# An RWKV-7 and GELU-MLP kernel: the two MLP products in other tile shapes of TensorE

## The chip, the core and the metric

The kernel runs on one core of one Trainium2 chip. The metric is the device time in microseconds of one execution on that core. TensorE does the matrix products into PSUM; VectorE (DVE), ScalarE (ACT) and GpSimd (POOL) do elementwise work; SyncE (SP) issues the DMAs.

## The reference

A recurrence over 768 steps for 4 x 8 heads of 40 channels, then an MLP on the 3072 tokens. All is fp32.

```python
for t in range(S):                       # S = 768; state is (B, H, D, D), D = 40
    y[:, :, t] = einsum('bhd,bhde->bhe', r[t], state)
    Sa = einsum('bhde,bhe->bhd', state, a[t])
    state = state * w[t] - Sa (outer) b[t] + v[t] (outer) k[t]
x = y as (3072 tokens, 320)              # B*S, H*D
h = x @ w_in                             # (3072, 2048)
g = h * (1 / (1 + exp(-1.702 * h)))
out = g @ w_out                          # (3072, 320)
```

## The kernel before

The sequence is cut into 12 chunks of 64 steps. A chunk has two units, each with two batches (p = 0, 1), so there are 24 units. For each unit the attention part forms decays, score products and a triangular solve by six doubling levels (`level`, tiles `ps_level`, `W`, `E`), then the output and the next state. Each level is a product of TensorE, an eviction by ScalarE or VectorE, and the next level waits for it. The unit's output goes through DRAM and comes back as `xT`, the transposed tokens for the MLP: 256 tokens of a chunk, 128 in each half.

The MLP of chunk c (`mlp`, L834) has these steps:

- `up(q, m, k)`: the 2048 hidden channels are 16 blocks of 128; q (four) and m (two) name a pair of blocks, r = 0, 1 one of the pair, and k one of five pieces of 64 of the 320 input channels. `w_in_sb` holds block r of a pair in row half r, and both row halves of `xT` hold the same 64 input channels of all 256 tokens. A task computes both blocks of its pair for one k; each block's 128 columns of weights are cut into two of 64, so that a task is four products of 64 rows by 64 columns with 256 moving columns. Block r has its own PSUM bank. There are 40 tasks a chunk.
- `gelu(q)`: one ScalarE activation of 128x1024 from PSUM into `g`.
- `down(p)`: for p = 0 and then p = 1, eight tasks `part(m)` sum over the 2048 hidden channels. The contraction of 128 rows is cut into two row halves, which go to the two banks of a PSUM pair; the 128 tokens are cut into two column halves. At the end a copy takes the first bank into `ob`, and a VectorE add brings in the second (L871, L873); then `store` issues two DMAs on SP.

In every product of the kernel the array stands as four 64x64 tiles, addressed in the order of `QUARTERS` (L243). A product in fp32 is two pairs of LDWEIGHTS and MATMUL instructions, so a task of four products with its loads has 16 instructions. All matmuls are issued by the helper `mm` (L270, L271 in the profile).

The program's order is written out by a planner (`Plan`, L59). A task has a rank, the engines that can run it and their costs in ns; `order` plays the five engines forward in time and takes for each free engine the ready task of lowest rank. Attention tasks have ranks below those of the MLP (10000 and more), so MLP tasks fill the time in which no attention task is ready. The planner also plays TensorE's instruction fetch in blocks of 256 (`fetched`, `ahead`): if the next task would run too far ahead of the fetch, it prefers a ready task with fewer instructions for its time. `paced` spreads the MLP tasks of a chunk over the time until the next chunk's. PSUM is handed out as four pairs of banks; `pair=(...)` names what holds a pair, and the last reader frees it. The number of buffers of each tile stands in one table (`g=4`, `ob=1`, `xT=3`).

Of the kernel before, what the change touches and what calls it, by code (L numbers as in the profile page):

```python
# [49 lines left out]

class Task:
    def __init__(self, rank, engines, fn, pair, most, size):
        self.instr, self.sbuf = engines.pop("instr", 0), engines.pop("sbuf", False)
        self.rank, self.fn, self.pair, self.most, self.size = rank, fn, pair, most, size
        self.engines = engines
        self.after, self.then, self.release = set(), [], 0.0


class Plan:  # L59
# [5 lines left out]
    BLOCK, FETCH, BESIDE, AHEAD = 256, 3550.0, 0.4, 300.0  # L65
    DELAY = {"PE": 300.0, "DVE": 60.0, "ACT": 60.0, "POOL": 150.0, "SP": 800.0}

    LATENCY, RATE, SPREAD = 1200.0, 400.0, 1.3

    def __init__(self, slots, pairs):  # L70
        self.slots, self.pairs = slots, pairs
# [25 lines left out]
    def order(self):  # L97
# [10 lines left out]
        able, now, wire, out, many = [], 0.0, 0.0, [], set()  # L108
# [8 lines left out]
                return clear > len({o.pair[0] for o in able if o.most is not None and o.pair not in held and not any(k[0] == o.pair[0] for k in many)})  # L117
            return clear > 0 and sum(k[0] == t.pair[0] for k in many) < t.most

        issued, begun, shared = 0, 0.0, 0.0  # L120

        def fetch(at):
            took = self.FETCH
# [9 lines left out]
        def fetched(t, start):  # L133

            at, left, ns, block = start, t.instr, t.engines["PE"] / t.instr, begun
            room = self.BLOCK - issued % self.BLOCK
            while left >= room:
                at += room * ns
                left -= room
                at = block = max(at, block + fetch(block))  # L140
                room = self.BLOCK
            return at + left * ns, block
# [5 lines left out]
        while coming or able:  # L148
            while coming and coming[0][0] <= now:
                able.append(self.tasks[heapq.heappop(coming)[1]])  # L150
            able.sort(key=lambda t: (t.rank, t.n))
            took = None
            for e in free:
                if free[e] <= now:
                    took = next((t for t in able if e in t.engines and fits(t) and unread(t, e) <= now), None)
                    if took and e == "PE" and ahead(took) > self.AHEAD:

                        took = next((t for t in able if e in t.engines and fits(t) and ahead(t) < min(self.AHEAD, ahead(took))), took)
                    if took:
                        break  # L160
            if not took:
                later = [x for x in (*free.values(), *pairs, *(unread(t, e) for t in able for e in t.engines)) if now < x < float("inf")]
                now = min(later + ([coming[0][0]] if coming else []))
                continue
            t = took
            able.remove(t)
            t.engine = e
            end = now + t.engines[e]
            if e == "PE":
                end, begun = fetched(t, now)  # L170
                issued += t.instr
            if e == "POOL" or e == "DVE" and t.sbuf:

                shared = max(now, shared) + t.engines[e]
                end = max(end, shared)
            free[e] = end
            if e == "SP":
                wire = max(wire, end + self.LATENCY)
                running.append((wire, wire + self.SPREAD * t.size / self.RATE))
                end = wire = running[-1][1]  # L180
            if t.pair is not None:
                if e != "PE":
                    last.setdefault(t.pair, {})[e] = end
                if t.pair not in held:
                    held[t.pair] = next(i for i, p in enumerate(pairs) if p <= now)
                    pairs[held[t.pair]] = float("inf")
                    if t.most is not None:
                        many.add(t.pair)
                t.bank = held[t.pair]
                users[t.pair] -= 1  # L190
                if not users[t.pair]:
                    many.discard(t.pair)
                    pairs[t.bank] = end + self.DELAY[e]
            for o in t.then:
                o.ready = max(o.ready, end + (0.0 if o.engines.keys() == {e} else self.DELAY[e]))
                o.left -= 1
                if not o.left:
                    heapq.heappush(coming, (max(o.ready, o.release), o.n))
            t.start = now
            out.append(t)  # L200
# [24 lines left out]
def rwkv7_gelu_quick(ctx: ExitStack, tc: tile.TileContext, time_d, v_d, w_d, wc_d, ak_d, b_d, rv_d, w_in, w_out, out):  # L225
    nc = tc.nc
    H, D, S = 8, 40, out.shape[0] // 4
    DM = H * D
# [3 lines left out]
    PIECE = w_in.shape[2]  # L232
    NF = w_in.shape[0] * PIECE // DM
    NM = NF // 2
    NK = DM // 64
    NQ = NM // 2
# [4 lines left out]
    HALF = [slice(0, 64), slice(64, 128)]  # L241
    BITS = (0, 1)
    QUARTERS = [(0, 0), (1, 1), (0, 1), (1, 0)]  # L243
# [5 lines left out]
    banks = ctx.enter_context(tc.tile_pool(name="banks", bufs=1, space=bass.MemoryType.PSUM))  # L249

    plan = Plan(dict(logw=3, wc=3, G=1, wch=3, wz=2, time=2, ak=2, b=2, rv=2, FT=3, GT=1, kh=2, bh=2, bz=2,
                     A=1, Av=1, RV=2, W=2, W0=2, W1=2, E=2, E0=2, E1=2, edge=1, zraw=2, zT=1, saT=1, M=2, y=1, x=1, xT=3, g=4, ob=1), 4)
    tiles, psums, drams = {}, {}, {}

    def single(name, shape):
# [9 lines left out]
    def psum(t, name):  # L265
        if t.pair not in psums:
            psums[t.pair] = banks.tile([128, 2, 512], FP32, tag=f"pair{t.bank}", name=name)
        return psums[t.pair]

    def mm(o, lhsT, rhs, start):  # L270
        nc.tensor.matmul(o, lhsT, rhs, start=start, stop=True, skip_group_check=True)  # L271
# [5 lines left out]
    def pe(*sets):  # L277

        return {"PE": sum(n * 2 * max(58.0, cols / 1.2 + 3) for n, cols in sets), "instr": sum(16 * n for n, _ in sets)}

    def dve(n):
        return {"DVE": 170.0 + 1.03 * n}
# [4 lines left out]
    def any2(n):  # L287
        return {**act(n), **dve(n)}

    def copy(e):  # L290
        return nc.scalar.copy if e == "ACT" else nc.vector.tensor_copy
# [22 lines left out]
    for p in HALF:  # L314
        q = slice(p.start, p.start + MID)
# [518 lines left out]
    def mlp(c):  # L834
        R = 10000 + 100 * c

        def up(q, m, k):
            def go(t):
                ph, x = psum(t, "ps_up"), xT_of(c)[:, :, k]
                for r, h in QUARTERS:  # L840
                    mm(ph[HALF[h], r, m * 256:(m + 1) * 256], w_in_sb[HALF[r], 2 * q + m, k, h * 64:(h + 1) * 64], x[HALF[r]],
                       m == 0 and k == 0)
            plan.add(R + q, pe((1, 256)), go, reads=[("xs", (c, p)) for p in BITS] + [("weight", q)],
                     uses=[("xT", c)], room=[("g", c * NQ + q)], pair=("up", c * NQ + q), most=1)

        def gelu(q):
            plan.add(-45, act(1024), lambda t: nc.scalar.activation(  # L847
                g_of(c * NQ + q).rearrange("p m r n -> p r m n"), psum(t, "").rearrange("p r (m n) -> p r m n", m=2),
                ACT.Gelu_apprx_sigmoid), writes=[("g", c * NQ + q)], pair=("up", c * NQ + q))

        def down(p):
            serial = 2 * c + p

            def part(m):
                def go(t):
                    po, g = psum(t, "ps_down"), g_of(c * NQ + m // 2)[:, m % 2]
                    for f in (2 * m, 2 * m + 1):
                        for r, b in QUARTERS:
                            o = p * 128 + b * 64
                            mm(po[HALF[b], r, :DM], g[HALF[r], f % 2, o:o + 64], w_out_sb[HALF[r], f * DM:(f + 1) * DM], f == 0)  # L860
                parts = range(2 * m * DM // PIECE, (2 * (m + 1) * DM - 1) // PIECE + 1)
                plan.add(R + 10 * (p + 1) + m, pe((2, 320)), go, reads=[("g", c * NQ + m // 2)] + [("weight", NQ + n) for n in parts],
                         pair=("down", serial), most=1)
            for m in range(NM):
                part(m)

            def store(t):
                for b in BITS:
                    o = (2 * p + b) * S + c * C
                    nc.sync.dma_start(out[o:o + C, :], ob_of(serial)[HALF[b]])  # L870
            plan.add(-45, any2(320), lambda t: copy(t.engine)(ob_of(serial), psum(t, "")[:, 0, :DM]),  # L871
                     writes=[("ob", serial)], pair=("down", serial))
            plan.add(-45, dve(320), lambda t: nc.vector.tensor_add(ob_of(serial), ob_of(serial), psum(t, "")[:, 1, :DM]),  # L873
                     reads=[("ob", serial)], writes=[("out", serial)], pair=("down", serial))
            plan.add(-100, {"SP": 700.0}, store, reads=[("ob", serial), ("out", serial)], size=128 * DM * 4)

        for q in range(NQ):
            for m in BITS:
                for k in range(NK):
                    up(q, m, k)  # L880
            gelu(q)
        for p in BITS:
            down(p)

    for i in range(3):
        load_w(i)
# [105 lines left out]
```

## Time and profile before

| what | value |
|---|---|
| two timed executions | 815.56 and 823.68 us, median 819.62 us |
| span of the profiled execution, first to last instruction | 816.7 us |
| its own time beside the span | not given apart; the span lies between the two timed executions |
| TensorE matmul busy, weight load busy | 749.6 us, 636.1 us, 24192 instructions each |
| VectorE, ScalarE, GpSimd busy | 477.7, 352.3, 153.3 us |
| granted TensorE clock, mean | 0.994 |
| up: matmul records, busy, mean of one | 3840, 274.5 us, 378 ns |
| down: matmul records, busy, mean of one | 3072, 243.8 us, 431 ns |
| instruction fetch (queue 8) | 190 packets, 3.11 MB |

In the profile PE is matmul and PEld is weight load. Matmuls are pipelined: a record's length holds the way through the array, and records of neighbouring matmuls lie over each other, so busy time is more than streaming time. The distance between the starts of successive matmuls on the same tile shows how long one occupies it. "issue" as the end of a wait means that the engine waited for nothing that the profile shows.

### The profile page before, as it was taken

The numbers are of one execution on the slowest core, as the hardware profiler recorded it, in microseconds if no ns is written. First come the engines' busy times: TensorE is split into PE (matmuls) and PEld (weight loads), VectorE is DVE, ScalarE is ACT, GpSimd is POOL, SyncE is SP. The second block draws the span as 40 slices with busy tenths as digits, with TensorE's granted clock in tenths as the row PEclk, the third lists the DMA queues.
The fourth block names the chain that finished last, engine by engine and source line by source line (L and its number), as shares of the span: only waits on it lengthen the run. The fifth ranks groups of instructions, "written<-read, shape, count | busy, mean of one in ns | idle before, by whom it ended". The sixth has DMA issues, their size and how long they took to land.

```text
span 816.7 us, 51357 instructions
## 1 busy us (share of the span) xinstructions
PE 749.6 (92%) x24192; PEld 636.1 (78%) x24192; DVE 477.7 (58%) x764; ACT 352.3 (43%) x603; POOL 153.3 (19%) x209
## 2 busy tenths in 40 slices
PE   4567887999999999999999989999999999999997
PEld 3556766787798888788888888887787887899785
DVE  7489778755755755756755654745556545455200
ACT  4376874444344253245254344355346345243210
POOL 4024052012202302302302302302103213200000
PEclk9899999999999999999999999999999999999999
DMA  9834452223403502412412512412403213110200
GB/s 348 329 110 146 136 194 72 70 69 89 134 17 91 152 20 86 133 45 82 138 45 68 152 44 74 141 46 72 142 15 98 71 50 92 40 33 4 60 10 18
DMA packets 32731, 76.31 MB, mean 93 GB/s; under 512 B 5096, under 2 KB 14312, under 8 KB 31496
## 3 DMA queue, kind: packets, MB, share of 16 engines
q1 hardware_dynamic: 32520, 73.03, 28.7%
q8 instruction: 190, 3.11, 1.6%
q14 instruction: 21, 0.17, 0.1%
HBM read 65.14 MB, written 7.86 MB: 89 GB/s over the span
## 4 chain that ended last, share of the span: by engine, by line
PE 79%; ACT 7%; DVE 6%; issue 4%; DMA 3%; SPq 1%; POOL 0%; ACTq 0%; DVEq 0%; POOLq 0%
PE ps_down L271 24%; PE ps_up L271 22%; PE ps_level L271 17%; PE ps_y L271 4%; PE ps_N L271 2%; ACT W L726 2%; PE ps_saT L271 1%; PE ps_Av L271 1%; PE ps_M L271 1%; PE ps_NT L271 1%; PE ps_A L271 1%; PE ps_RV L271 1%; PE ps_rz L271 1%; ACT L847 1%; PE ps_zT L271 1%
## 5 line engine op out<-in xcount | busy, mean ns | idle before, releaser
L271 PE MATMUL ps_up<-xT,w_sb 64*64 64x256 f32 x3840 | 274.5, 378 | 7.6 <-issue 4.5
L271 PE MATMUL ps_down<-w_sb,g 64*64 64x320 f32 x3072 | 243.8, 431 | 2.9 <-DVE w_sb L406 1.6
L726 ACT COPY W<-ps_level 128x672 f32<-128x672 f32 (+1 forms) x164 | 102.4, 626 | 184.2 <-PE ps_level L271 176.7
L271 PEld LDWEIGHTS ps_up<-xT,w_sb 64*64 64x64 f32 x3840 | 159.9, 134 | 27.3 <-issue 7.2
L271 PEld LDWEIGHTS ps_level<-W,E 64*64 64x64 f32 x5888 | 153.0, 134 | 27.9 <-issue 4.5
L271 PEld LDWEIGHTS ps_down<-w_sb,g 64*64 64x64 f32 x3072 | 130.9, 133 | 43.8 <-DVE w_sb L406 2.0
L271 PE MATMUL ps_level<-W,E 64*64 64x64 f32 (+2 forms) x5888 | 152.2, 230 | 7.8 <-issue 2.5
L721 DVE TENSOR_TENSOR E<-twice,ps_level 128x512 f32<-128x512 f32 x120 | 81.8, 686 | 87.8 <-ACT W L726 75.6
L538 POOL TENSOR_TENSOR kh<-time,G 128x320 f32<-128x320 f32 x23 | 20.8, 906 | 414.5 <-issue 289.3
L271 PE MATMUL ps_level<-W 64*64 64x64 f32 (+2 forms) x2560 | 69.4, 239 | 22.1 <-issue 10.3
L271 PEld LDWEIGHTS ps_level<-W 64*64 64x64 f32 x2560 | 66.2, 138 | 29.5 <-issue 15.0
L847 ACT ACTIVATE g<-ps_up 128x1024 f32<-128x1024 f32 x48 | 49.2, 1026 | 42.6 <-PE ps_up L271 42.2
L812 POOL TENSOR_TENSOR x<-y,FT 128x128 f32<-128x128 f32 x88 | 56.1, 667 | 0.7 <-DVE y L802 0.4
L705 DVE TENSOR_TENSOR W<-edge,ps_level 128x672 f32<-128x672 f32 x40 | 33.9, 850 | 12.2 <-PE ps_level L271 11.1
L530 POOL TENSOR_TENSOR ak<-ak,FT 128x512 f32<-128x512 f32 x20 | 27.9, 1394 | 64.1 <-DMA ak<-in_ak 55.8
L873 DVE TENSOR_TENSOR ob<-ob,ps_down 128x320 f32<-128x320 f32 x24 | 11.6, 482 | 48.0 <-ACT ob L871 45.7
L271 PE MATMUL ps_y<-RV,kh 64*64 64x104 f32 x768 | 37.1, 251 | 1.3 <-issue 1.3
L271 PE MATMUL ps_y<-M,bh 64*64 64x104 f32 x768 | 37.5, 250 | 0.5 <-issue 0.4
L726 DVE COPY W<-ps_level 128x672 f32<-128x672 f32 (+1 forms) x36 | 26.4, 733 | 14.2 <-PE ps_level L271 14.1
L271 PEld LDWEIGHTS ps_y<-RV,kh 64*64 64x64 f32 x768 | 29.0, 133 | 4.6 <-issue 2.9
L767 DVE TENSOR_TENSOR M<-ps_M,upper 128x512 f32<-128x512 f32 x24 | 16.6, 690 | 26.5 <-PE ps_M L271 26.4
L716 DVE TENSOR_TENSOR E<-twice,ps_level 128x256 f32<-128x256 f32 x40 | 16.8, 420 | 26.1 <-ACT W L726 16.9
(114 smaller groups left out, 986.0 us busy)
## 6 DMA issues: line engine op xcount, KB each, us to landing
time<-in_time SPq DMA_DIRECT2D x24, 480.0 KB
xT<-x_dram SPq DMA_DIRECT2D x48, 160.0 KB
ak<-in_ak SPq DMA_DIRECT2D x44, 160.0 KB
rv<-in_rv SPq DMA_DIRECT2D x44, 160.0 KB
wc<-in_wc SPq DMA_DIRECT2D x24, 264.0 KB
extra<-in_w_out SPq DMA_DIRECT2D x4, 1280.0 KB
logw<-in_w SPq DMA_DIRECT2D x24, 160.0 KB
RV<-in_v SPq DMA_DIRECT2D x24, 160.0 KB
```

The source lines that it names most:

```text
L271: nc.tensor.matmul(o, lhsT, rhs, start=start, stop=True, skip_group_check=True)
L530: plan.add(R, {"DVE": 690.0, "POOL": 1270.0, "sbuf": True}, lambda t: of(t.engine).tensor_mul(ahT(), ahT(), FT_of(i)), reads=T("ak", "FT") ...
L538: plan.add(R + 4, {"POOL": 870.0, "DVE": 490.0, "sbuf": True}, lambda t, n=n, dst=dst: of(t.engine).tensor_mul(dst(i)[:, :, :D], by_head(t ...
L705: plan.add(key, dve(672), lambda t: nc.vector.tensor_sub(W_of(s + 2)[:, :, b], edge[:, :, b], item(t)[:, :, :, :168]), reads=T("edge"), wr ...
L716: plan.add(key, dve(256), lambda t: nc.vector.tensor_tensor(E_of(es + 2)[:, :, b, :, 64:], wide(ident if early else twice).to_broadcast([1 ...
L721: plan.add(key, dve(512), lambda t: nc.vector.tensor_sub(E_of(es + 2)[:, :, b].rearrange("p h j (n t) -> p h (j n) t", n=2), wide(twice).t ...
L726: plan.add(key, any2(4 * (168 - lo)), lambda t: copy(t.engine)(W_of(s + 2)[:, :, b, :, lo:], item(t)[:, :, :, lo:168]), writes=keeps, pair ...
L767: plan.add(R + 4, dve(512), lambda t: nc.vector.tensor_tensor(M_of(i)[:, :, :64].rearrange("p (e j) t -> p e j t", e=2), psum(t, "")[:, :, ...
L812: of(t.engine).tensor_mul(x[:, b ^ u, b], y_of()[:, at], FT_of(i)[:, at])
L847: plan.add(-45, act(1024), lambda t: nc.scalar.activation(g_of(c * NQ + q).rearrange("p m r n -> p r m n"), psum(t, "").rearrange("p r (m ...
L873: plan.add(-45, dve(320), lambda t: nc.vector.tensor_add(ob_of(serial), ob_of(serial), psum(t, "")[:, 1, :DM]), reads=[("ob", serial)], wr ...
```

## The change

Up: the four 64x64 products of a task become two products of 64 rows by 128 columns, one for each row half. Down: the products over two row halves and two token halves become one product of 128 rows by 128 columns; the row halves are no longer summed apart, so the VectorE add goes. Both token halves p are done in one task, which holds one PSUM pair with one p in each bank, and each p is copied to `ob` and stored on its own. `ob` gets a second buffer. The planner learns a mode for each task (64 for attention, 65 for up, 128 for down), charges 200 ns where the mode changes, and gets the new numbers of instructions.

```diff
-    LATENCY, RATE, SPREAD = 1200.0, 400.0, 1.3
+    LATENCY, RATE, SPREAD, SWITCH = 1200.0, 400.0, 1.3, 200.0
...
             if e == "PE":
-                end, begun = fetched(t, now)
+                end, begun = fetched(t, now + (self.SWITCH if t.mode != mode else 0.0))
+                mode = t.mode
                 issued += t.instr
...
-                     A=1, Av=1, RV=2, W=2, W0=2, W1=2, E=2, E0=2, E1=2, edge=1, zraw=2, zT=1, saT=1, M=2, y=1, x=1, xT=3, g=4, ob=1), 4)
+                     A=1, Av=1, RV=2, W=2, W0=2, W1=2, E=2, E0=2, E1=2, edge=1, zraw=2, zT=1, saT=1, M=2, y=1, x=1, xT=3, g=4, ob=2), 4)
...
-                for r, h in QUARTERS:
-                    mm(ph[HALF[h], r, m * 256:(m + 1) * 256], w_in_sb[HALF[r], 2 * q + m, k, h * 64:(h + 1) * 64], x[HALF[r]],
-                       m == 0 and k == 0)
-            plan.add(R + q, pe((1, 256)), go, reads=[("xs", (c, p)) for p in BITS] + [("weight", q)],
+                for r in BITS:
+                    mm(ph[:, r, m * 256:(m + 1) * 256], w_in_sb[HALF[r], 2 * q + m, k], x[HALF[r]], m == 0 and k == 0)
+            plan.add(R + q, {**pe((1, 256)), "instr": 8, "mode": 65}, go, reads=[("xs", (c, p)) for p in BITS] + [("weight", q)],
...
-        def down(p):
+        def down(m):
+            def go(t):
+                po, g = psum(t, "ps_down"), g_of(c * NQ + m // 2)[:, m % 2]
+                for f, p in product((2 * m, 2 * m + 1), BITS):
+                    mm(po[:, p, :DM], g[:, f % 2, p * 128:(p + 1) * 128], w_out_sb[:, f * DM:(f + 1) * DM], f == 0)
+            parts = range(2 * m * DM // PIECE, (2 * (m + 1) * DM - 1) // PIECE + 1)
+            plan.add(R + 10 + m, {"PE": 4 * 2 * (320 / 1.2 + 3), "instr": 16, "mode": 128}, go,
+                     reads=[("g", c * NQ + m // 2)] + [("weight", NQ + n) for n in parts], pair=("down", c), most=1)
+
+        def store(p):
             serial = 2 * c + p
-            def part(m):
-                def go(t):
-                    po, g = psum(t, "ps_down"), g_of(c * NQ + m // 2)[:, m % 2]
-                    for f in (2 * m, 2 * m + 1):
-                        for r, b in QUARTERS:
-                            o = p * 128 + b * 64
-                            mm(po[HALF[b], r, :DM], g[HALF[r], f % 2, o:o + 64], w_out_sb[HALF[r], f * DM:(f + 1) * DM], f == 0)
...
-            plan.add(-45, any2(320), lambda t: copy(t.engine)(ob_of(serial), psum(t, "")[:, 0, :DM]),
-                     writes=[("ob", serial)], pair=("down", serial))
-            plan.add(-45, dve(320), lambda t: nc.vector.tensor_add(ob_of(serial), ob_of(serial), psum(t, "")[:, 1, :DM]),
-                     reads=[("ob", serial)], writes=[("out", serial)], pair=("down", serial))
-            plan.add(-100, {"SP": 700.0}, store, reads=[("ob", serial), ("out", serial)], size=128 * DM * 4)
+            plan.add(-45, any2(320), lambda t: copy(t.engine)(ob_of(serial), psum(t, "")[:, p, :DM]),
+                     writes=[("ob", serial)], pair=("down", c))
+            plan.add(-100, {"SP": 700.0}, go, reads=[("ob", serial)], size=128 * DM * 4)
```

## The prediction

> **What bounds the kernel now.** I read the page's engine rows and slices first, then the stretches of time, then the TensorE groups by form, then the chain near the end, then the timeline of one stretch.
>
> ```profile
> PE 749.6 (92%) x24192; PEld 636.1 (78%) x24192; DVE 477.7 (58%) x764; ACT 352.3 (43%) x603; POOL 153.3 (19%) x209
> PE   4567887999999999999999989999999999999997
> q8 instruction: 190, 3.11, 1.6%
> ```
> TensorE is the fullest engine, and from the eighth slice (about 150 us) to the end it is never below 8 tenths. Before that VectorE, ScalarE and DMAs set the pace (weights and inputs arrive). Queue 8 fetches instructions: 2 x 24192 TensorE instructions over 190 packets are 255 each.
>
> ```profile
> 0.00:150.00 150.00, 105.30 (x3888) 90.50 (x3892) 115.56 (x153) 91.04 (x146) 45.74 (x62) 0.97 0.54 187
> 150.00:770.00 620.00, 602.16 (x19628) 514.54 (x19624) 359.98 (x606) 255.83 (x450) 107.55 (x147) 1.00 0.26 76
> 770.00:817.00 47.00, 42.14 (x692) 31.05 (x684) 2.17 (x7) 5.38 (x7) 0.00 (x0) 0.99 0.10 26
> ```
> Columns: stretch, its length, busy time of PE, PEld, DVE, ACT, POOL, clock, DMA share, GB/s. Start-up, a middle with attention and MLP mixed, and a tail of the last chunk's MLP alone. Busy PE is not streaming PE, so I price the middle by rounds:
>
> ```profile
> L271 PE MATMUL ps_up<-xT,w_sb 64*64 64x256 f32 x3840 | 274.5, 378 | 7.6 <-issue 4.5 <-DMA xT<-x_dram 1.6 <-PE ps_A L271 0.5
> L271 PE MATMUL ps_down<-w_sb,g 64*64 64x320 f32 x3072 | 243.8, 431 | 2.9 <-DVE w_sb L406 1.6 <-DVE ob L873 0.7 <-DVE M L767 0.3
> L271 PE MATMUL ps_M<-rv,saT 64*64 64x64 f32 x768 | 17.8, 222 | 0.3 <-issue 0.3
> L271 PEld LDWEIGHTS ps_down<-w_sb,g 64*64 64x64 f32 x3072 | 130.9, 133 | 43.8 <-DVE w_sb L406 2.0 <-issue 1.6 <-DVE ob L873 0.9
> ...
> 787.36 4.32 PE ps_up L271 x80
> 791.67 1.08 PE ps_down L271 x16
> 792.75 4.32 PE ps_up L271 x80
> 797.07 15.11 PE ps_down L271 x224
> ```
> Every fp32 product is two MATMUL records, and four 64x64 tiles run as one round. The chain's last pieces, free of attention, give 4.32/(80/4) = 216 ns a round of up and 15.11/(224/4) = 270 ns of down; the trace's starts of 64-column rounds lie 58 ns apart, of 104-column ones 89. Counted so, the middle holds 173 us of up, 170 of down and 240 of attention: 583 of its 620 us. **Only 37 us there are lost**, whatever their cause. By the starts in the trace about 30 of the 37 stand where the first MLP round follows attention, where instruction fetch has to catch up (packets of queue 8 come 3.9 us apart in the middle by median and 3.4 at the dense end, 13 ns an instruction; a solve level's 64 instructions stream in only 0.3 us).
>
> ```profile
> 408.49 1.05 PE L271 MATMUL ps_up<-xT,w_sb 64*64 64x256 f32 x16
> 409.36 0.77 PE L271 MATMUL ps_level<-W,E 64*64 64x104 f32 x32
> 409.95 0.61 PE L271 MATMUL ps_up<-xT,w_sb 64*64 64x256 f32 x8
> 410.38 0.77 PE L271 MATMUL ps_level<-W,E 64*64 64x104 f32 x32
> 410.97 1.05 PE L271 MATMUL ps_up<-xT,w_sb 64*64 64x256 f32 x16
> 411.83 0.77 PE L271 MATMUL ps_level<-W,E 64*64 64x104 f32 x32
> ```
> This timeline (start, length, PE group, records) is the line that decides: the planner fills each latency of the solve with one or two MLP tasks. Counting such stretches through the middle gives 359 of attention, 229 of up and 139 of down. Today all are 64x64, so the alternation is free: the step from up or down to attention costs a median of 0 ns over streaming.
>
> **What the Trainium skill says.** "TensorEngine Tiling (Array Packing)", Tiling Modes, Key Properties: "Changing tiling mode (not just tile) drains the TensorE", and it lists 64x64, 64x128 and 128x128 as separate configurations. No run here shows a change yet. "TensorE: Matmul & The Clock Gate", Part 3, lets weight loads overlap running matmuls only where the row group differs; this trace disagrees, since rounds of four tiles that fill all rows still come every 270 ns though each reloads its own tile (133 ns a load). The same page, LDWEIGHTS, makes a load columns/1.2 ns: 53 ns for 64 columns and 107 for 128, so I estimate 133 + 54 = 187 ns for the new loads. "Runtime: NRT & Kernel Launch", Instruction fetch mechanics, gives blocks of 256 instructions; 255 per packet here agrees.
>
> **The change, part by part.**
> Streaming: an up task was two rounds of four quarter tiles (432 ns) and becomes two rounds of two 64x128 tiles with the same 256 columns, 432 ns. A down step was two tasks (one for each p) of four rounds, 8 x 270 = 2.16 us, and becomes eight full matmuls of 320 columns, again 2.16 us. Gain 0. A load of 187 ns fits under 216 or 270 ns of streaming if it is preloaded as today.
>
> Instructions: up has 480 tasks and drops from 16 to 8 instructions each (-3840); down has 192 tasks of 32 and becomes 96 of 16 (-4608). That is 8448 of 48384, or 33 packets fewer. Fetch demand falls from 190 x 3.4 = 646 us to about 534, so it no longer competes with PE. It can return at most the 37 us; bounds 0 and 37. I take 33, since a drain also covers what is left of such waits.
>
> Mode switches, the new cost: each change among attention, up and down. The trace can't show one, so I bound it. From above: the last record's pipeline beyond its streaming (429 - 270 = 159, 378 - 216 = 162), then a full new load of 187: 350 ns. From below, 0 if these modes need no drain, or 55 if only the preloading is lost: after a wait at 703.03 us the first load precedes the first matmul by 20 ns and that round's records last 249 ns instead of 218, 51 together. The middle reading, drain plus restart, is 160 + 55 = 215; [...]I take 180. The 200 that the diff gives the planner is an input of the planner and no measurement.
>
> How many: now 727 stretches in the middle. A down task is twice as long and there are half as many: about 85 visits instead of 139. Up tasks keep their size, about 400 in the middle at 1.75 a visit: 229 or a little fewer, since after each dear visit more of the solve is ready and attention runs longer. Visits then are 290 (240 if attention bunches more, 360 if up tasks fall one at a time); each has a switch in and a switch out: 580 (480 to 720). The tail has a few, start-up under 50, which hide under its own waits. 580 x 0.18 = 104 us. It lies on the path, as nothing in the middle is later than PE.
>
> VectorE and ScalarE: the 24 adds of 0.49 us into ob (L873) go, 11.6 us on an engine that is 58% busy: 0 on the path except at the end, where copy 0.43 and add 0.49 in a row become two copies side by side: -0.5. With ob at two buffers and one PSUM pair for both p instead of two in turn, nothing is added to the path. The two stores stay two DMAs each on SP; the removed wait of the add on the copy has only VectorE work behind it. Buffers g come free earlier, as one down task reads both p; up's row shows 1.6 us of waits for xT and none for g, so I book 0.
>
> Sum on the span: 816.7 + 104 - 33 - 0.5 = 887. The page gives no time outside the span; the two timed runs (815.56 and 823.68) enclose it and their median is 2.9 above. **Forecast 890 us**, own range 840 to 955.
>
> **The rivals.**
> *Free modes, fetch relief counts* (ends faster): the row and column masks of different sizes coexist, a switch costs 0, and the 37 us return nearly whole: 816.7 - 33.5 + 2.9 = 786. For it: the 8448 instructions and the stalls behind attention are real, and loads are seen to run ahead. Against: the skill's drain, and that the array holds weights of the old shape.
> *Lost preload only*: a switch costs 55 ns; 580 x 0.055 = 32 against 33.5 back: 818, no change. The point between the signs is 33.5/580 = 58 ns a switch.
> *Loads are not hidden in full-array mode*: with no second tile to work meanwhile, each of 768 matmuls waits 187 ns: 144 us more on top of the forecast, 1034. For it: the page's sentence on row groups; against: same-tile preloading in this trace.
> *The new shapes don't do what they say*: two 64x128 tiles that run one after the other would add 960 x 0.216 = 207 us. Against: four tiles run side by side today.
>
> **How the numbers follow.** Forecast by switches 0.68; free modes 0.16; lost preload 0.11; the two exposures 0.05. Slower by over 2% takes the first and last except a cheap edge of 0.03: 0.70. Within 2%, which is about what a measurement of this kernel can tell from no change, 0.14; faster by over 2% 0.16. The range takes in the free-mode case from 785 and the forecast's own upper end, 955; outside are the exposures, half of the free case, and the dearest switches, some 0.18.
>
> **What would show each step.** Up should have 1920 MATMUL records and down 768, with a mean near 378 and 430 ns; rounds in the tail 216 and 270 ns (longer: exposed loads). Queue 8 should have about 157 packets. Where attention meets MLP the gap between last and first matmul should exceed streaming by 150 to 210 ns; under 60 and I am wrong on the sign. The middle should be longer by 60 to 80 us, start-up unchanged, the tail within 1 us. If the stretches number under 350 while the gaps are as priced, it is the count that failed.

## The result and the profile after

The changed kernel takes 912.38 us (median of 910.32 and 914.45) against 819.62: the ratio is 1.111, 95% interval 1.101 to 1.121. It is slower, as forecast; the forecast was 890 us. The profiled execution has a span of 908.6 us, 91.9 more than before. Every ratio below is taken against the kernel before as it ran beside that kernel (medians of 818 to 822 us).

The page's engine rows, the PE slices and the fetch queue:

```profile
PE 858.3 (94%) x19968; PEld 640.4 (70%) x19968; DVE 452.9 (50%) x719; ACT 398.5 (44%) x656; POOL 145.1 (16%) x201
PE   4669999999999989999999999999999998999997
q8 instruction: 157, 2.57, 1.2%
```

There are 8448 fewer TensorE instructions and 33 fewer fetch packets, as worked out, yet PE's busy time grew by 109 us, and its share of the span rose from 92% to 94%. Read alone, that would look like an improvement. The TensorE groups by form say what the busy time is made of (operation, tile rows*columns, records, busy us, mean ns of one):

```profile
L272 PE MATMUL ps_up<-xT,w_sb 64*128 64x256 f32 x1920 | 284.7, 409 | 7.2 <-ACT g L847 4.3 <-issue 1.6 <-DVE E L708 0.9
L272 PE MATMUL ps_down<-w_sb,g 128*128 128x320 f32 x768 | 228.9, 444 | 0.0
L272 PEld LDWEIGHTS ps_up<-xT,w_sb 64*128 64x128 f32 x1920 | 164.9, 188 | 41.7 <-issue 7.6 <-ACT g L847 4.7 <-PE ps_level L272 1.0
L272 PEld LDWEIGHTS ps_down<-w_sb,g 128*128 128x128 f32 x768 | 139.1, 189 | 58.1 <-issue 5.6 <-DVE x L813 0.3
L272 PEld LDWEIGHTS ps_level<-W,E 64*64 64x64 f32 x5888 | 115.9, 134 | 59.1 <-issue 47.4 <-DVE E L722 5.3 <-ACT G L502 2.5
```

The last group as it was before:

```profile
L271 PEld LDWEIGHTS ps_level<-W,E 64*64 64x64 f32 x5888 | 153.0, 134 | 27.9 <-issue 4.5 <-DVE E L721 3.7 <-ACT g L847 2.8
```

The new loads last 188 and 189 ns, as estimated (187). The means 409 and 444 are above the 378 and 431 of before. A visit here is an unbroken run of up, of down or of attention in the order of TensorE, and a round is one step of all tiles of the mode together. Most records didn't get longer: in the trace an up record inside a visit lasts 376 ns and only the first round of each visit 480; for down it is 433 and 537. The second round starts later by the same 104 ns. So the first matmul after a change of mode waits 104 ns for its load, and 83 visits of down spread over 768 records give 433 + 83 x 104 / 768 = 444, the mean on the page. For an attention round of 64 moving columns the first lasts 267 instead of 218 ns, some 50 more for its load of 64 weight columns. The last row shows the other side: PEld stood idle for 47.4 us before solve levels while it "waited for nothing that the profile shows". Before, that entry was 4.5.

The timeline of one visit there and back (start, length, engine, group, records):

```profile
410.20 0.38 PE L272 MATMUL ps_up<-xT,w_sb 64*128 64x256 f32 x1
410.24 1.28 ACT L847 ACT_TABLE_LOAD   x1
410.50 0.56 PEld L272 LDWEIGHTS ps_A<-ak 64*64 64x64 f32 x32 [0.33 <-issue]
410.50 0.69 PE L272 MATMUL ps_A<-ak 64*64 64x64 f32 x32
411.06 0.68 SPq L823 DMA_DIRECT2D x_dram<-x  x2
411.13 0.95 PEld L272 LDWEIGHTS ps_up<-xT,w_sb 64*128 64x128 f32 x10
411.13 1.13 PE L272 MATMUL ps_up<-xT,w_sb 64*128 64x256 f32 x8
```

No weight load starts before the mode has changed: the loads of ps_A start at 410.50 with its first matmul, those of up at 411.13 with theirs. Before, loads of the next task ran under the old task's matmuls:

```profile
408.73 0.81 PE L271 MATMUL ps_up<-xT,w_sb 64*64 64x256 f32 x10
409.14 0.46 PEld L271 LDWEIGHTS ps_level<-W,E 64*64 64x64 f32 x12
409.36 0.36 PE L271 MATMUL ps_level<-W,E 64*64 64x104 f32 x8
```

Here the solve level's loads start at 409.14, and its first matmul, without delay, at 409.36. Back in the changed kernel, the last round of ps_A starts at 410.96 in the trace and streams 58 ns; up begins 110 ns after that. This gap is what the text calls the drain. It is almost constant: the medians beyond streaming are 110 ns from attention to up or down, 97 from up to attention, 92 from down to attention, 96 and 93 between up and down. With the exposed load of the first round (104 or 50) a visit costs 110 + 104 + 97 + 50 = 361 ns for up and 356 for down.

The stretches of the changed kernel (length, busy PE, PEld, DVE, ACT, POOL, clock, DMA share, GB/s), with the mixed middle now ending at 866 us:

```profile
0.00:150.00 150.00, 117.20 (x3505) 95.66 (x3506) 112.90 (x153) 85.45 (x138) 42.25 (x60) 0.93 0.55 188
150.00:866.00 716.00, 704.03 (x16236) 516.98 (x16235) 340.03 (x567) 307.47 (x510) 102.87 (x141) 1.00 0.22 66
866.00:909.00 43.00, 37.09 (x230) 27.80 (x228) 0.00 (x0) 5.60 (x8) 0.00 (x0) 0.97 0.07 16
```

Start-up streams 89.5 us in its 150 (88.2 before), so it lost nothing. The middle streams 588 of 716 us by the same count of rounds: 128 us are lost where 37 were.

The tail's cut at 866 falls later in the work than that at 770 before. At the same work, the start of the last chunk's long run of up, the chains have these pieces, before and after:

```profile
777.65 8.63 PE ps_up L271 x160
```

```profile
867.40 8.83 PE ps_up L272 x80
```

So up to there the kernel takes 90 us longer, and from there to the end of the span 2 us.

### The profile page after: what moved, and what is told of

It reads as the page before. It is cut to its first block, busy times and chain, and to the rows that moved or that the text cites. A ratio compares the mean times of both kernels' runs of the same rounds, so it can differ in the third digit from the quotient of the medians.

```text
span 908.6 us, 42913 instructions
## 1 busy us (share of the span) xinstructions
PE 858.3 (94%) x19968; PEld 640.4 (70%) x19968; DVE 452.9 (50%) x719; ACT 398.5 (44%) x656; POOL 145.1 (16%) x201
## 4 chain that ended last, share of the span: by engine, by line
PE 82%; ACT 8%; issue 1%; DVE 0%; POOL 0%; ACTq 0%
PE ps_up L272 27%; PE ps_down L272 23%; PE ps_level L272 16%; PE ps_y L272 4%; PE ps_N L272 2%; PE ps_M L272 1%; PE ps_zT L272 1%; PE ps_A L272 1%; PE ps_saT L272 1%; ACT L847 1%; PE ps_rz L272 1%; PE ps_NT L272 1%; PE ps_Av L272 1%; PE ps_RV L272 1%; ACT g L847 1%
## 5 line engine op out<-in xcount | busy, mean ns | idle before, releaser
L272 PE MATMUL ps_up<-xT,w_sb 64*128 64x256 f32 x1920 | 284.7, 409 | 7.2 <-ACT g L847 4.3
L272 PE MATMUL ps_down<-w_sb,g 128*128 128x320 f32 x768 | 228.9, 444 | 0.0
L272 PEld LDWEIGHTS ps_up<-xT,w_sb 64*128 64x128 f32 x1920 | 164.9, 188 | 41.7 <-issue 7.6
L727 ACT COPY W<-ps_level 128x672 f32<-128x672 f32 (+1 forms) x172 | 106.9, 628 | 194.4 <-PE ps_level L272 167.5
L272 PEld LDWEIGHTS ps_down<-w_sb,g 128*128 128x128 f32 x768 | 139.1, 189 | 58.1 <-issue 5.6
L272 PEld LDWEIGHTS ps_level<-W,E 64*64 64x64 f32 x5888 | 115.9, 134 | 59.1 <-issue 47.4
L272 PE MATMUL ps_level<-W,E 64*64 64x64 f32 (+2 forms) x5888 | 136.0, 235 | 5.5 <-ACT G L502 1.7
L272 PEld LDWEIGHTS ps_level<-W 64*64 64x64 f32 x2560 | 58.2, 139 | 33.1 <-issue 24.0
L631 DVE TENSOR_TENSOR W<-ps_N,lower 128x512 f32<-128x512 f32 x24 | 16.5, 689 | 35.4 <-PE ps_N L272 35.3
L575 ACT COPY Av<-ps_Av 128x320 f32<-128x320 f32 x20 | 8.5, 425 | 58.5 <-PE ps_Av L272 58.4
```

Of the source, the lines that this page charges most:

```text
L575: plan.add(R + 1, any2(320), lambda t: copy(t.engine)(Av_of(i).rearrange("p e b n -> p b e n"), psum(t, "")[:, :, :160].rearrange("p b (e ...
L631: plan.add(R, dve(512), lambda t: nc.vector.tensor_tensor(first()[:, :, :, :64], get(t)[:, :, :, :64], mask(lower), ALU.mult), writes=halv ...
L727: plan.add(key, any2(4 * (168 - lo)), lambda t: copy(t.engine)(W_of(s + 2)[:, :, b, :, lo:], item(t)[:, :, :, lo:168]), writes=keeps, pair ...
```

## The experiments

The theory: a change of mode costs a drain and an exposed load, and the time is that price times the number of changes. Rivals: the full-array products are dear in themselves; or the new order and its 200 ns charge, not the array, cost the time. The number of changes is counted in each kernel's TensorE order: the changed kernel has 690, with 273 visits of up and 83 of down. In the diffs "..." marks what is left out.

**Down alone at full array** (from the changed kernel):

```diff
-                for r in BITS:
-                    mm(ph[:, r, m * 256:(m + 1) * 256], w_in_sb[HALF[r], 2 * q + m, k], x[HALF[r]], m == 0 and k == 0)
-            plan.add(R + q, {**pe((1, 256)), "instr": 8, "mode": 65}, go, ...
+                for r, h in QUARTERS:
+                    mm(ph[HALF[h], r, m * 256:(m + 1) * 256], w_in_sb[HALF[r], 2 * q + m, k, h * 64:(h + 1) * 64], x[HALF[r]],
+                       m == 0 and k == 0)
+            plan.add(R + q, pe((1, 256)), go, ...
```

> Only the down product is changed (full array, one task for both token halves, no add); up stays at 64x64. Switch theory (each mode change costs a drain of about 100 ns and then an exposed first load, 0.36 us for a visit there and back): the planned order has 88 visits of down, so 88 x 0.36 = 31 us more and, with 4608 instructions fewer, perhaps 20 us of the 37 us lost in the middle back: about 828 us span, ratio 1.01 (0.99 to 1.03). Full-array theory (the 128x128 products themselves are the dear part, by loads that don't hide): at least half of the 92 us stays, 863 or more. Order theory (the new plan, not the modes, costs the time): near 900.

Measured: 845.66 us, ratio 1.029 (1.022 to 1.037). That is the upper edge of the switch theory and well below the other two. Most of the 20 us of fetch relief that were expected did not appear; the kernels with down alone and no charge, and with long down tasks at 64x64, below, take this apart.

**Up alone at 64x128**, with down, its add and `ob` as in the kernel before (from the changed kernel):

```diff
-        def down(m):
-            def go(t):
-                po, g = psum(t, "ps_down"), g_of(c * NQ + m // 2)[:, m % 2]
-                for f, p in product((2 * m, 2 * m + 1), BITS):
...
+        def down(p):
+            serial = 2 * c + p
...
+                        for r, b in QUARTERS:
```

> Only the up product is changed (64 rows by 128 columns); down stays at 64x64 with its add. Switch theory: the planned order has 251 visits of up, 251 x 0.36 = 90 us more, and about 33 us of lost time come back because the drains cover it: about 874 us, ratio 1.07 (1.05 to 1.09). Full-array theory: little more than before, 820 to 840, since up is not at full array. Order theory: near 900.

Measured: 867.40 us, ratio 1.056 (1.047 to 1.064), as the switch theory had it (1.05 to 1.09). The product that isn't at full array costs more than the one that is: the full-array theory falls, and at 867 the order theory ("near 900") does not fit either.

**The changed order, up in quarters**: the planner sees the changed kernel, but the up task issues the four 64x64 products.

```diff
-                for r in BITS:
-                    mm(ph[:, r, m * 256:(m + 1) * 256], w_in_sb[HALF[r], 2 * q + m, k], x[HALF[r]], m == 0 and k == 0)
+                for r, h in QUARTERS:
+                    mm(ph[HALF[h], r, m * 256:(m + 1) * 256], w_in_sb[HALF[r], 2 * q + m, k, h * 64:(h + 1) * 64], x[HALF[r]],
+                       m == 0 and k == 0)
```

> The order of every engine is that of the changed kernel; only the up products are issued as four 64x64 quarters again, so that attention and up share one mode. Switch theory: 83 visits of down remain, 83 x 0.36 = 30 us, some of the fetch relief is lost: 825 to 840 us, ratio 1.01 to 1.03. Order theory (the planner charged 200 ns for switches and so moved the work badly): stays above 880, ratio 1.07 or more.

Measured: 886.78 us, ratio 1.079 (1.071 to 1.087): a miss for the switch theory and what the order theory expected. In its trace the steps from attention to up are back at a median of 0 ns, so these changes of mode really are gone, but waits of over 0.4 us between attention products total 69 us over the whole span, where the changed kernel has 33. An order planned around 200 ns charges, and around 8 instructions per up task, is not free when the array doesn't pay the charge.

The kept traces say what many of these waits are. Take TensorE's waits of over 0.1 us in the mixed middle (the step from one matmul's start to the next, less streaming and the price of a change), and look at how long before its end a packet of queue 8, the instruction fetch, had last ended. In the kernel before, 38 of 60 such waits, 18 of 27 us, end between 1.0 and 1.75 us after a packet; by chance it would be a fifth of them. In the changed kernel it is 4 of 32, 1 of 16 us, which is no more than chance. In this one it is 62 of 122, 40 of 60 us. So TensorE waited mostly for instructions here: up has 16 per task again, in an order that was planned for 8. This is a reading of times that coincide; no run varied the fetch alone. The next two runs look at the charge.

**No charge in the planner**:

```diff
-    LATENCY, RATE, SPREAD, SWITCH = 1200.0, 400.0, 1.3, 200.0
+    LATENCY, RATE, SPREAD, SWITCH = 1200.0, 400.0, 1.3, 0.0
```

> The changed kernel with SWITCH at 0 in the planner: both new shapes, the order planned as if a mode change were free; 674 changes of mode instead of 690. Switch theory: the array pays by the number of changes, 674 against 690, so 905 to 915 us, the same as the changed kernel within 1%. Order theory (charging 200 ns made the order bad): clearly faster than the changed kernel, 880 or less.

Measured: 910.79 us, ratio 1.115 (1.108 to 1.122), against 912.38 for the changed kernel. The charge is not what makes the changed kernel slow.

**The charge alone**: the products of before, with the charge and mode labels for the planner only.

```diff
-    LATENCY, RATE, SPREAD = 1200.0, 400.0, 1.3
+    LATENCY, RATE, SPREAD, SWITCH = 1200.0, 400.0, 1.3, 200.0
...
-            plan.add(R + q, pe((1, 256)), go, ...
+            plan.add(R + q, {**pe((1, 256)), "mode": 65}, go, ...
...
-                plan.add(R + 10 * (p + 1) + m, pe((2, 320)), go, ...
+                plan.add(R + 10 * (p + 1) + m, {**pe((2, 320)), "mode": 128}, go, ...
```

> The products of the kernel before (all 64x64, honest instruction counts), but ordered by the planner that charges 200 ns wherever attention, up and down change. No change of mode exists on the array. Switch theory: no switch, so near before; the plan puts less MLP between solve levels than it could, which I put at 0 to 25 us: 820 to 845. Order theory: the charge explains the 887 us of the kernel that had the changed order with up in quarters, so 870 or more. If this one is near before, that kernel lost its time to instruction fetch, since its order was planned with 8 instructions per up task and ran 16.

Measured: 857.26 us, ratio 1.048 (1.042 to 1.054), between the two expectations. A charge that the array doesn't levy costs 37 us. Its waits that follow a fetch packet make up 32 us, against 18 before, so some 14 of the 37 are of that kind; the rest stays open. The 37 us agree with the miss above: with 83 visits of down at 0.36 us = 30, on 820, they make 887. It is a sum that fits and not a separate proof; the wrong instruction count of that kernel was not tested alone. When the charge is real, as in the changed kernel, the order with and without it ends at the same time.

**Coarser up tasks**: both new shapes, but all five k in a task.

```diff
-        def up(q, m, k):
+        def up(q, m):
             def go(t):
-                ph, x = psum(t, "ps_up"), xT_of(c)[:, :, k]
-                for r in BITS:
-                    mm(...)
+                for k in range(NK):
+                    x = xT_of(c)[:, :, k]
+                    for r in BITS:
+                        mm(...)
```

> Both new shapes, but an up task holds all five k (2.16 us instead of 0.43), so the planned order changes mode 344 times instead of 690. Switch theory: about 62 us of switches instead of 138, less 33 us of lost time that comes back: about 846 us, ratio 1.03 (1.01 to 1.06; above if the coarse tasks keep the solve waiting). Full-array or per-product theory: the number of products is that of the changed kernel, so 900 or more.

Measured: 858.75 us, ratio 1.045 (1.037 to 1.052), with the same products and 344 changes instead of 690. The by-form group of up in this kernel:

```profile
L272 PE MATMUL ps_up<-xT,w_sb 64*128 64x256 f32 x1920 | 236.9, 389 | 7.7 <-DVE W L727 2.5 <-DMA xT<-x_dram 2.4 <-ACT g L849 2.4
```

Same records, 48 us less busy, the mean down from 409 to 389. Half of the changes removed gave 54 us back, 155 ns each.

**More changes in the same order**: in each down step the second token half is issued as two tiles of 128 rows by 64 columns, side by side.

```diff
-                    mm(po[:, p, :DM], g[:, f % 2, p * 128:(p + 1) * 128], w_out_sb[:, f * DM:(f + 1) * DM], f == 0)
+                    for h in HALF if p else [slice(0, 128)]:
+                        mm(po[h, p, :DM], g[:, f % 2, p * 128 + h.start:p * 128 + h.stop], w_out_sb[:, f * DM:(f + 1) * DM], f == 0)
```

> The changed kernel in its own order, but in each down step the products of the second token half are issued as two tiles of 128 rows by 64 columns, so that the mode changes three times inside each of 96 tasks: 301 changes more, nothing else moved, 768 PE instructions more (under 2% of them). Switch theory: 301 x (0.093 + about 0.077) = 51 us more, about 963 us, ratio to before 1.17. Theories without a price for a change of mode (order, fetch): 912 to 920. If two column tiles don't run side by side, another 100 us on top.

Measured: 954.60 us, ratio 1.167 (1.161 to 1.173): 42 us for 301 changes, 140 ns each, with nothing else moved. That is 9 us less than expected; its waits of over 0.1 us in the middle fell from 16 to 12 us, which is about half of that. The chain at the end, first of the changed kernel and then of this one (start, us, group, records), shows the full price, because there is no attention beside it:

```profile
885.46 4.52 PE ps_up L272 x40
889.98 13.13 PE ps_down L272 x48
```

```profile
925.95 4.52 PE ps_up L272 x40
930.47 17.12 PE ps_down L272 x72
```

Six down steps with 3 changes inside each and 5 between them: (17.12 - 13.13) / 23 = 173 ns each. This is near the 174 that the gaps and first loads in this trace average for the two directions. Theories without a price for a change had 912 to 920.

**Blocks of down**: up at 64x64, four down steps in one task.

```diff
-        for m in range(NM):
-            down(m)
+        for m in range(0, NM, 4):
+            down(range(m, m + 4))
```

> Up at 64x64 as before; down at full array, but four of its steps (8.6 us) in one task, so 24 visits instead of 88. Switch theory: 24 x 0.36 = 9 us instead of 31 us in the kernel with down alone changed; 4608 instructions fewer: 820 to 832 us, ratio 1.00 to 1.015, if the solve can wait 8.6 us. If long tasks starve the solve: above 846.

Measured: 894.59 us, ratio 1.094 (1.087 to 1.101): only 24 visits, and 49 us slower than with 88. The switch theory's 820 to 832 held only if the solve can wait 8.6 us. Its waits of PE name what came late:

```profile
PE ps_level L272 <- issue: 19.3, 16, 3.7
PE ps_up L272 <- DMA xT<-x_dram: 18.4, 10, 4.2
```

Up waited 18.4 us for xT, 5.1 in the kernel with 88 visits and 1.6 before. The likely reading is that while TensorE is in a block of 8.6 us the solve stands, its output comes late, and the MLP has nothing to fill with. A second part is instruction fetch: the waits that follow a fetch packet make up 40 us here and 15 in the kernel with 88 visits, so that attention without MLP tasks between its products may also run short of instructions. The two were not tested apart.

**Down alone, no charge**, and **long down tasks at 64x64** (no mode change at all):

```diff
-    LATENCY, RATE, SPREAD, SWITCH = 1200.0, 400.0, 1.3, 200.0
+    LATENCY, RATE, SPREAD, SWITCH = 1200.0, 400.0, 1.3, 0.0
```

```diff
-            def part(m):
+            def part(q):
...
-                    for f in (2 * m, 2 * m + 1):
+                    for f in range(4 * q, 4 * q + 4):
                         for r, b in QUARTERS:
```

> Down alone at full array, as in the kernel with down alone changed (846 us), but the planner charges nothing for a change of mode: 89 visits of down, the same price on the array. Switch theory: 840 to 850, the same. If the charge put the solve's work badly there, as it did in the kernel with the charge alone (857 against 820 us): nearer 830, that is 31 us of switches less the fetch relief.

> All products at 64x64 as before, no charge, but a down task holds four of the 128-channel blocks instead of two, so it lasts 2.16 us like the new one, in 84 visits instead of 147. It isolates what the longer task costs by itself. Switch theory: no change of mode, so 815 to 830. If the longer task is what costs in the kernel with down alone changed: about 845.

Measured: 837.50 us, ratio 1.024 (1.019 to 1.029), and 835.38 us, ratio 1.020 (1.014 to 1.025). Both lie between what was expected, and neither is clear of 2%. So a down task of 2.16 us costs some 16 us by itself, with 84 visits and no mode change. The full array differs from it by 2 us, which is inside the scatter, though its 89 visits are worth 32 us. If the two costs add, some 30 us come back from elsewhere. The fetch queue of these two, full array first, shows what else differs:

```profile
q8 instruction: 172, 2.82, 1.4%
```

```profile
q8 instruction: 190, 3.11, 1.5%
```

The 18 packets fewer explain a part of the 30 us at most: the waits that follow a fetch packet make up 11 us at full array and 20 at 64x64, a difference of 9. The other waits of over 0.1 us fell from 23 to 14. The remaining 13 us or so stay open. With the charge the down kernel takes 8 us more (845.66), the rest of its excess.

## Why the prediction was right, and where its size was off

- *Direction and mechanism*: right. The drain that the Trainium skill states ("TensorEngine Tiling (Array Packing)", Key Properties) is there, for each pair of the three modes, and it has a price here: 92 to 110 ns, and then a load that is not preloaded, 50 or 104 ns. The time goes with the number of changes: 344 instead of 690 gave 54 us back, and 301 more took 42.
- *Price of a change*: 180 ns was taken, below a middle reading of 215. In the middle the medians give 113 us over 625 changes, 180 each. That the sum agrees to the nanosecond is luck. The two halves were otherwise than argued: the drain is 92 to 110 ns and not the 160 of the pipeline, and the exposed load is up to 104 and not about 50. The gap alone was forecast at 150 to 210 ns and missed that.
- *Streaming*: unchanged as booked. Up rounds stay at 216 ns and down matmuls at 269; loads of 188 ns hide within a mode. That includes the full array, where each load goes under a matmul that fills all rows, so the row-group sentence of "TensorE: Matmul & The Clock Gate", Part 3, is contradicted here too.
- *Number of changes*: the first mis-sized term. 580 were taken in the middle, 625 came. The prediction's own parts, 229 visits of up and 85 of down, make 314; it took 290, because it expected attention to bunch after each dear visit. It didn't bunch: 246 visits of up and 73 of down came, 319. That is 8 us.
- *Relief*: the second. The waits in the middle fell from 37 to 128 - 113 = 15 us, so 21 or 22 came back and not 33. That is 12 us. 887 + 8 + 12 = 907, against 908.6. The relief was argued from instruction fetch, and this was right for a part of the 37 us only: the waits that follow a fetch packet fell from 18 us to 1, as good as all of them, while the other waits of over 0.1 us rose from 9 to 15. The reading that some 30 of the 37 us stand where MLP follows attention does not come out of the starts either: counted again tile by tile, some 11 us stand there, and the larger part between one attention product and the next. Nor does a solve level's 64 instructions stream in 0.3 us; the level at 409.36 takes 0.59.
- *Its signs*: the middle was to grow by 60 to 80 us and the tail by at most 1. At the same work they grew by 90 and 2.
- *A term not in the sum*: the longer down task got no price, and the run with long tasks at 64x64 shows 16 us. In the changed kernel it can't be told apart from the term above, because what the drains cover and what the longer tasks add stand in the same waits. That the sum nearly closes hides this.
- *Rivals*: free modes, lost preload only, loads that don't hide, and tiles that run in turn all fall by the rows above.

Whether some version of the change beats both kernels stays open: none of the ten was faster than the kernel before. In them fewer changes came with longer tasks, and the longest ones kept the solve waiting.

## What to carry to other kernels

Before reshaping TensorE tiles for part of a kernel, count in the timeline how often that part alternates with the rest: here each change of mode cost a drain and an exposed load, 0.18 us together, and no engine total of the profile before showed it. The 690 changes cost more than the saving of a sixth of TensorE's instructions gave back. Grouping the work to change less often helped from 0.43 to 2.16 us per up task, and hurt where a down task held 8.6 us. Compare waits with the ends of the fetch packets, too: it tells which of them fewer instructions can remove.

## What was not expected of the hardware

- The drain hardly depends on what is drained: 92 to 110 ns after matmuls of 64 to 320 columns, and the next start comes before the old records' modelled tail of 160 ns (376 less 216) is over.
- Two tiles of 128 rows by 64 columns do run side by side. One after the other they would have added 12 products of two 269 ns rounds, 6.5 us, to the last chain of that kernel; it grew by 3.99 us, and 23 changes at the gaps and loads of its trace account for 4.0.
- Where TensorE ran short of instructions in the kernel before, it mostly went on 1.0 to 1.75 us after a fetch packet's end (38 of 60 waits). The order of the same instructions decides how often: the charge alone raised these waits from 18 to 32 us.
